# Attention visits between FFN steps regrouped into fewer and longer ones, and the transpose of q moved behind the sums

## Chip, cores and metric

One core of a Trainium2 chip. The metric is the device time of one execution in microseconds (us); a median and the range of a kernel's runs are given. All runs used here count as fast, with a mean granted TensorE clock of 0.992 to 1.0. Two of the traces, those of e1 and e2, hold a stretch of 3.4 us at half clock while PE works, and it matters below.

## The reference

Linformer attention feeds a max-out FFN. Eight batches, eight heads, sequence 1024, head size 64, 64 projected keys; then 8192 tokens of 512 go through three 512 x 768 matrices and one 768 x 512.

```python
k_proj = einsum('ks,bhsd->bhkd', E, k);  v_proj = einsum('ks,bhsd->bhkd', F, v)
attn = softmax(q @ k_proj^T / 8);        x = attn @ v_proj     # per batch and head
h = max(x @ w1, x @ w2, x @ w3);         out = h @ w_out
```

## The kernel before

TensorE (PE) runs the FFN of batch `b` as a loop of two halves, each of ten steps: 0 to 5 are "up" (12 matmuls of 128x128 by 512 columns), 6 to 9 "down" (6 such). The attention of the next batch `n = b + 1` is done in **visits** between those steps. A plan says which work stands behind which (half, step).

All PSUM is eight banks. The kernel deals them out; a score, sum or value unit takes a pair:

```python
    psum_t = psum.tile([P, 8, 512], FP32, name="banks")
    ...
    def two():                                  # a pair: 0-1, 2-3, 4-5 or 6-7
        n = min(range(0, 8, 2), key=lambda n: max(free[n:n + 2]))
    ...
    def bank():                                 # one bank: up, down, projections
        n = min(range(8), key=lambda n: free[n])
```

The pieces of a visit (cut):

```python
    sc(b, g)    # scores of head pair g: 4 matmuls 64x64 into a pair; ACT empties it with exp -> pT
    zc(b)       # column sums of all four pT; ACT makes 1/sum (zic); store to DRAM (zd),
                # four broadcast loads back (zi_all), all on the SyncE queue
    vx(b, g)    # values of pair g: 4 matmuls 64x64 into a pair; DVE empties it, times zi_all -> xT
    kproj(b), vproj(b)   # k, v projections, one bank each;  kt(b): transpose of k's, a pair
    qd(b)       # q: four copies on DVE (q_p), then one DMA transpose on the SyncE queue -> qT
    ld(b)       # loads of q, k, v; that of q waits until the transpose of the batch before landed
```

With `now=True` the exponential is put on ACT at once; otherwise it is put there after the next step's own copy. An up step takes three banks one after the other; ACT copies the first out, DVE takes the maxima with the second and third.

The plan from batch 3 on, before the change:

```python
        out = {
            (0, 1): [sc(n, 1, now=True), sc(n, 2, now=True), sc(n, 3)],
            (0, 3): [zc(n)],
            (1, 2): [vx(n, 0), vx(n, 1)],
            (1, 6): [vx(n, 2), vx(n, 3)],
        }
        if n + 1 < B:
            out[0, 2] = [qd(n + 1)]
            out[1, 2] = [kproj(n + 1), vproj(n + 1)] + out[1, 2]
            out[1, 3] = [kt(n + 1)]
            out[1, 6] += [sc(n + 1, 0)]
```

No visit has more than three units.

The softmax here doesn't subtract the row's maximum and nothing guards it: scores larger than these inputs give would overflow.

Of the kernel before, what the change touches and what calls it, by code (L numbers as in the profile page):

```python
# [15 lines left out]
def kernel(  # L16
# [15 lines left out]
    B, H, S, D = q.shape  # L32
# [10 lines left out]
    NPAIR = H // 2  # L43
# [38 lines left out]
    def bank():  # L82
        n = min(range(8), key=lambda n: free[n])
        deal((n,))
        return psum_t[:, n, :], (n,)

    def pe(dt, wait=0.0):
        clock["pe"] = max(clock["pe"], wait) + dt
        return clock["pe"]

    def runs(eng, ready, dt, ns=()):
        if eng in clock:
            clock[eng] = max(clock[eng], ready + 0.06) + dt
            for n in ns:
                free[n] = clock[eng]
            return clock[eng]
        return ready + dt
# [145 lines left out]
    def zi_all(b):  # L243
        if b not in zi_alls:
            zi_alls[b] = att.tile([P, NPAIR, 2, CHUNK], FP32, name="zi_all", bufs=1)
        return zi_alls[b]

    def zc(b):



        def f():
            t, ns = bank()
            for hp in range(2):
                for g in range(NPAIR):
                    nc.tensor.matmul(  # L256
                        out=t[32 * g:32 * (g + 1), :], lhsT=pick[:, hp, :],
                        rhs=pTs[b, g, 0][:, hp, :], start=(hp == 0), stop=(hp == 1),
                    )
            ready = pe(2 * MM + 0.1)  # L260
            zlc = att.tile([P, CHUNK], FP32, name="zlc", bufs=1)
            nc.scalar.activation(out=zlc, in_=t, func=AF.Ln)
            runs("s", ready, 0.6, ns)
            zic = att.tile([P, CHUNK], FP32, name="zic", bufs=1)
            nc.scalar.activation(out=zic, in_=zlc, func=AF.Exp, scale=-1.0)
            when = runs("s", ready, 0.63) + 9.0
            zd = scratch.tile([NPAIR, 2, 2, CHUNK], FP32, name="zd")
            nc.sync.dma_start(
                out=zd.rearrange("g h c f -> (g h c) f"),
                in_=zic.rearrange("(a r) f -> a r f", r=8)[:, 0, :],  # L270
            )
            for u in range(2):
                gs = slice(2 * u, 2 * u + 2)
                for hp in range(2):
                    nc.sync.dma_start(
                        out=zi_all(b)[hp * HALF:(hp + 1) * HALF, gs],
                        in_=zd[gs, hp].partition_broadcast(HALF),
                    )
            for g in range(NPAIR):
                zis[b, g, 0] = zi_all(b)[:, g], when  # L280
        return f

    def vx(b, g):
        def f():
            scale_x(b, g, 0, SI, values(b, g, 0, SI))
        return f
# [13 lines left out]
    def values(b, g, lo, nsi):  # L300
        if b not in xTs:
            xTs[b] = att.tile([P, NCT, SI, P], BF16, name="xT")
        return pair_mm(b, g, lo, nsi, lambda rows, hp: vps[b][rows, 2 * g + hp, :])
# [17 lines left out]
    def sc(b, g, lo=0, nsi=SI, now=False):  # L321
        def f():
            t = scores(b, g, lo, nsi)
            if now:
                exps(b, g, lo, nsi, t)
            else:
                later.append(lambda: exps(b, g, lo, nsi, t))
        return f

    def za(b, g, lo=0, nsi=SI, then=False):  # L330
        def f():
            z = sums(b, g, lo, nsi)
            av = values(b, g, lo, nsi)
            invert(b, g, lo, nsi, z)
            if then:
                later.append(lambda: scale_x(b, g, lo, nsi, av))
            else:
                scale_x(b, g, lo, nsi, av)
        return f
# [40 lines left out]
    def qd(b, parts=1):  # L380

        def f():
            q_p = att.tile([P, NPAIR, SI, 2, D], BF16, name="q_p", bufs=1)
            qTs[b] = att.tile([P, NPAIR * SI, P], BF16, name="qT")
            n = NPAIR // parts
            for lo in range(0, NPAIR, n):
                for g in range(lo, lo + n):
                    copy(
                        "v", q_p[:, g].rearrange("p si h d -> p h si d"),
                        qkv[b][0][:, 2 * g:2 * g + 2], (), 0.43,  # L390
                    )
                last_T[b] = nc.sync.dma_start_transpose(
                    out=qTs[b][:, lo * SI:(lo + n) * SI, :],
                    in_=q_p[:, lo:lo + n].rearrange("p g si h d -> p (g si h d)"),
                )
        return f

    kps = {}
    def kproj(b):
        def f():  # L400
            t, ns = bank()
            proj(b, 1, t, (LO, HI), 4 * D)
            kps[b] = att.tile([P, 2, 2 * D], BF16, name="kp")
            copy("v", kps[b].rearrange("a g x -> a (g x)"), t[:, 0:4 * D], ns, 0.43)
        return f

    def kt(b):
        def f():
            t, ns = two()
            t = t.bitcast(BF16)[:, 0]  # L410
            for gg in range(2):
                nc.tensor.transpose(
                    out=t[:, gg * P:(gg + 1) * P], in_=kps[b][:, gg, :], identity=ident
                )
            pe(0.2)

            kpTs[b] = att.tile([P, NPAIR, KP], BF16, name="kpT")
            copy(
                "v", kpTs[b].rearrange("a (y x) k -> a x y k", x=2),
                t[:, 0:2 * P].rearrange("a (x y k) -> a x y k", x=2, y=2), ns, 0.3,  # L420
            )
        return f

    def vproj(b):
        def f():
            t, ns = bank()
            proj(b, 2, t, (LO, HI), 4 * D)

            vps[b] = att.tile([P, H, D], BF16, name="vp")
            for hh, hs in enumerate((LO, HI)):  # L430
                i = t[hh * HALF:(hh + 1) * HALF, 0:4 * D].rearrange("a (h d) -> a h d", d=D)
                for to in range(2):
                    copy("sv"[hh], vps[b][to * HALF:(to + 1) * HALF, hs, :], i, ns, 0.4)
        return f
# [250 lines left out]
    def plan(b):  # L685
        n = b + 1
        if b == 0:
            c1 = (SPC, SPC)
            return {
                (0, 6): [za(0, 1, *c1), sc(0, 3, *c1)],  # L690
                (0, 7): [qd(1, 2), za(0, 2, *c1)],
                (0, 8): [za(0, 3, *c1)],
                (1, 0): [kproj(1)],
                (1, 1): [kt(1)],
                (1, 2): [vproj(1), ld(2)],
                (1, (3, "mid")): [sc(1, 0), sc(1, 1)],
                (1, 4): [za(1, 0), sc(1, 2)],
                (1, 5): [za(1, 1), sc(1, 3)],
                (1, 7): [za(1, 2)],
                (1, 8): [za(1, 3)],  # L700
            }
        if b == 1:
            return {
                (0, 1): [qd(2)],
                (0, 5): [kproj(2), vproj(2), ld(3)],
                (0, 6): [kt(2)],
                (0, 7): [sc(2, 0)],
                (0, 9): [za(2, 0), sc(2, 1)],
                (1, 1): [za(2, 1), sc(2, 2)],
                (1, 3): [za(2, 2), sc(2, 3)],  # L710
                (1, 5): [za(2, 3)],
                (1, 6): [qd(3)],
            }
        if b == 2:
            return {
                (0, 0): [kproj(3), vproj(3), ld(4)],
                (0, 1): [kt(3)],
                (0, 2): [sc(3, 0, now=True), sc(3, 1)],
                (0, 4): [sc(3, 2, now=True), sc(3, 3)],
                (0, 6): [zc(3)],  # L720
                (0, 7): [qd(4)],
                (1, 3): [kproj(4), vproj(4), ld(5), vx(3, 0), vx(3, 1)],
                (1, 4): [kt(4)],
                (1, 6): [vx(3, 2), vx(3, 3), sc(4, 0)],
            }
        if n == B:
            return {}
        out = {
            (0, 1): [sc(n, 1, now=True), sc(n, 2, now=True), sc(n, 3)],
            (0, 3): [zc(n)],  # L730
            (1, 2): [vx(n, 0), vx(n, 1)],
            (1, 6): [vx(n, 2), vx(n, 3)],
        }
        if n + 1 < B:
            out[0, 2] = [qd(n + 1)]
            out[1, 2] = [kproj(n + 1), vproj(n + 1)] + out[1, 2]
            out[1, 3] = [kt(n + 1)]
            out[1, 6] += [sc(n + 1, 0)]
        if n + 2 < B:
            out[1, 3] += [ld(n + 2)]  # L740
        return out
# [61 lines left out]
```

## Time and profile before

| | before |
|---|---|
| time, median (range) | 404.61 us (403.92 to 404.71, 3 runs) |
| profiled span | 402.6 us |
| PE busy / DVE / ACT | 97% / 50% / 39% |
| batch 3, 4, 5, 6 (from first FFN weight load to the next batch's) | 47.59, 46.49, 46.72, 44.29 us |

PE is the bound, so what counts is each interval in which the FFN matmuls do not follow each other at 0.216 us. I read these intervals from single starts of weight loads, of which none is missing in the trace (2311), while 43 matmul records are. The view below is the timeline of the kernel before at (1,6) of batch 5 (start, length, engine, line, operation, tiles, count, idle time before and what ended it). Two value units and one score follow each other, and the FFN goes on at once. (In all timelines shown, rows that the reading doesn't need, mostly weight loads, are left out.)

```profile
308.66 0.63 PE L231 MATMUL banks<-pT,vp 64*64 64x512 bf16 x8
308.77 0.58 ACT L102 COPY o_sb<-banks 128x512 f32<-128x512 f32 x1 [2.67 <-PE banks L664]
309.12 0.39 PE L211 MATMUL banks<-qT,kpT 64*64 64x512 bf16 x4
309.66 0.81 PE L664 MATMUL banks<-wout_sb,hT 128*128 128x512 bf16 x3 [0.16 <-issue]
```

The 0.16 before the last line is a missing record: the weight load that belongs to it starts at 309.43.

### The profile page before, as it was taken

What the parts mean: (1) busy time and instruction counts of PE and PEld (TensorE: products, weight loads), DVE (VectorE), ACT (ScalarE), POOL (GpSimd) and SP (SyncE); (2) the same over time, 40 slices, a digit from 0 to 9 for tenths busy, and PEclk for the clock granted to TensorE, in tenths of its full rate; (3) what the DMA queues carried; (4) which work ended last, traced back from release to release, by engine and by line L of the source; (5) the groups of instructions that cost most, each with busy time, mean ns of one, the idle gap of its engine ahead of it and who ended that gap; (6) DMA issues with size and microseconds to landing.
All of it is one profiled execution on the core that took longest, in us unless ns stands there. A gap on an engine that the chain in (4) does not pass through costs nothing.

```text
span 402.6 us, 5752 instructions
## 1 busy us (share of the span) xinstructions
PE 389.0 (97%) x2268; PEld 177.0 (44%) x2311; DVE 203.2 (50%) x319; ACT 155.8 (39%) x244; POOL 31.4 (8%) x44
## 2 busy tenths in 40 slices
PE   7899999999999999999999999999999999999996
PEld 3444444344445445444444445444454444444443
DVE  2347754762655425836264534746167342745251
ACT  2431537624763452253323532245322533132322
POOL 7350002002000200200010000100000000000000
PEclk9999999999999999999999999999999999999999
DMA  9999999969917999999899779983860229020202
GB/s 150 203 205 207 225 208 144 229 156 135 255 30 186 153 187 213 214 221 203 156 244 248 180 152 244 243 202 62 181 180 2 105 51 261 5 106 0 104 2 104
DMA packets 65707, 63.98 MB, mean 159 GB/s; under 512 B 30528, under 2 KB 58688, under 8 KB 65680
## 3 DMA queue, kind: packets, MB, share of 16 engines
q0 software_dynamic: 28512, 28.31, 43.9%
q1 hardware_dynamic: 37024, 35.16, 33.4%
q8 instruction: 18, 0.29, 0.3%
q10 hardware_dynamic: 144, 0.13, 0.1%
q14 instruction: 9, 0.07, 0.1%
HBM read 67.63 MB, written 16.94 MB: 210 GB/s over the span
## 4 chain that ended last, share of the span: by engine, by line
PE 85%; DMA 5%; DVE 3%; ACT 3%; issue 2%; POOL 0%; SPq 0%; DVEq 0%; ACTq 0%; POOLq 0%
PE banks L567 56%; PE banks L664 18%; PE banks L345 3%; PE banks L231 3%; DMA zi_all<-zd 3%; DMA k_t<-in_k_dram 2%; PE banks L211 2%; DVE xT L308 2%; ACT zl L291 1%; ACT zi_all L297 1%; PE banks L256 1%; DVE hT L577 1%; ACT pT L222 1%; DMA zd<-zic 1%; PE banks L470 1%
## 5 line engine op out<-in xcount | busy, mean ns | idle before, releaser
L567 PE MATMUL banks<-xT,w_sb 128*128 128x512 bf16 x1119 | 254.7, 379 | 2.8 <-issue 1.1
L567 PEld LDWEIGHTS <-w_sb 128*128 128x128 bf16 x1152 | 109.8, 98 | 137.5 <-issue 10.1
L629 DVE TENSOR_TENSOR m<-banks,h1s 128x512 f32<-128x512 f32 x90 | 62.1, 690 | 125.9 <-ACT h1s L625 81.1
L625 ACT COPY h1s<-banks 128x512 f32<-128x512 f32 x90 | 52.6, 584 | 112.2 <-PE banks L567 109.3
L664 PE MATMUL banks<-wout_sb,hT 128*128 128x512 bf16 x369 | 85.6, 379 | 1.3 <-issue 0.8
L577 DVE TENSOR_TENSOR hT<-banks,m 128x512 bf16<-128x512 f32 x90 | 62.3, 692 | 10.7 <-PE banks L567 1.7
L664 PEld LDWEIGHTS <-hT 128*128 128x128 bf16 x378 | 35.7, 98 | 47.4 <-issue 4.8
L102 ACT COPY o_sb<-banks 128x512 f32<-128x512 f32 (+1 forms) x56 | 32.6, 582 | 58.5 <-PE banks L664 58.3
L308 DVE TENSOR_TENSOR xT<-banks,zi_all 128x1024 bf16<-128x1024 f32 x28 | 33.3, 1221 | 22.5 <-ACT zi_all L297 17.0
L222 ACT ACTIVATE pT<-banks 128x1024 bf16<-128x1024 f32 (+1 forms) x36 | 32.8, 932 | 24.1 <-PE banks L211 24.1
L200 POOL DMA_DIRECT2D q_t<-in_q_dram x7 | 6.1, 878 | 189.9 <-DMA qT<-q_p 87.0
L291 ACT ACTIVATE zl<-banks 128x512 f32<-128x512 f32 (+1 forms) x16 | 13.0, 810 | 9.8 <-PE banks L231 8.9
L345 PEld LDWEIGHTS <-efT 128*64 128x64 bf16 x224 | 11.6, 110 | 3.4 <-issue 3.0
L102 DVE CAST vp<-banks 64x256 bf16<-64x256 f32 (+1 forms) x18 | 7.1, 397 | 10.9 <-ACT vp L102 7.8
L102 ACT CAST vp<-banks 64x256 bf16<-64x256 f32 x14 | 5.1, 364 | 19.0 <-PE banks L345 18.9
L231 PE MATMUL banks<-pT,vp 64*64 64x512 bf16 (+1 forms) x144 | 11.8, 362 | 0.4 <-DVE vp L102 0.4
L211 PE MATMUL banks<-qT,kpT 64*64 64x512 bf16 (+1 forms) x144 | 11.5, 361 | 0.0
L102 DVE COPY q_p<-q_t 128x1024 bf16<-128x1024 bf16 x28 | 10.0, 419 | 0.0
L297 ACT ACTIVATE zi_all<-zl 128x1024 f32<-128x1024 f32 x8 | 8.5, 1057 | 0.3
L102 DVE COPY o_sb<-banks 128x512 f32<-128x512 f32 (+1 forms) x9 | 5.8, 653 | 4.5 <-PE banks L644 4.5
L441 PE MATMUL banks<-warm_f 128*128 128x512 f32 x8 | 6.6, 977 | 1.5 <-DVE warm_f L175 1.5
L200 POOL DMA_DIRECT2D k_t<-in_k_dram x7 | 6.1, 878 | 20.2 <-PE banks L345 19.9
(59 smaller groups left out, 119.7 us busy)
## 6 DMA issues: line engine op xcount, KB each, us to landing
out_dram<-o_sb SPq DMA_DIRECT2D x30, 512.0 KB, 6.8
zi_all<-zd SPq DMA_DIRECT2D x20, 512.0 KB, 8.6
q_t<-in_q_dram POOLq DMA_DIRECT2D x7, 1024.0 KB, 13.4
k_t<-in_k_dram POOLq DMA_DIRECT2D x7, 1024.0 KB, 15.8
v_t<-in_v_dram POOLq DMA_DIRECT2D x7, 1024.0 KB, 20.1
w_sb<-in_moe_w_dram POOLq DMA_DIRECT2D x5, 384.0 KB, 11.7
k_t<-in_k_dram POOLq DMA_DIRECT2D x2, 512.0 KB, 10.7
v_t<-in_v_dram POOLq DMA_DIRECT2D x4, 256.0 KB, 13.3
```

Of the source, the lines that this page charges most:

```text
L102: done = {"v": nc.vector.tensor_copy, "s": nc.scalar.copy, "g": nc.gpsimd.tensor_copy}[eng](out=o, in_=i)
L211: nc.tensor.matmul(out=t[c * HALF:(c + 1) * HALF, hp, 0:n * P], lhsT=kpTs[b][rows, g, :], rhs=qTs[b][rows, at:at + n, :], start=True, stop ...
L222: nc.scalar.activation(out=pTs[b, g, lo], in_=t, func=AF.Exp, scale=scale)
L231: nc.tensor.matmul(out=t[hp * HALF:(hp + 1) * HALF, c, 0:nsi * HALF], lhsT=w(rows, hp), rhs=p[rows, hp, :], start=True, stop=True,)
L291: nc.scalar.activation(out=zl, in_=t, func=AF.Ln)
L308: nc.vector.tensor_tensor(out=xTs[b][:, g, lo:lo + nsi, :].rearrange("a (c s) p -> a c (s p)", c=2), in0=t, in1=zi, op=ALU.mult,)
L345: nc.tensor.matmul(out=t[hh * HALF:(hh + 1) * HALF, 0:width], lhsT=efT[:, si, (kv - 1) * KP:kv * KP], rhs=qkv[b][kv][:, heads[hh], si, :], ...
L567: nc.tensor.matmul(out=h, lhsT=w_sb[i][:, ct, jt * P:(jt + 1) * P], rhs=xTs[b][:, ct, ch * SPC:(ch + 1) * SPC, :], start=(ct == first), st ...
L577: nc.vector.tensor_tensor(out=o, in0=h, in1=other, op=ALU.max)
L625: nc.scalar.copy(out=h1s, in_=h[0][0])
L629: nc.vector.tensor_tensor(out=m12, in0=h[1][0], in1=h1s, op=ALU.max)
L664: nc.tensor.matmul(out=o_ps, lhsT=hTs[b, ch][:, jt, tt * P:(tt + 1) * P], rhs=wout_sb[:, jt, :], start=(jt == 0), stop=(jt == NJT - 1),)
```

## The change

The intent: fewer visits, since each costs a fixed price. From batch 5 on the four scores are made in one visit, at (1,6) of the batch before; three of the four value units go together behind the k and v projections; the last batch's four value units are one visit; two visits of batch 0 become one; and the transpose of q goes behind the sums, so that the reciprocals go first on the SyncE queue.

```diff
-                (1, 7): [za(1, 2)],
-                (1, 8): [za(1, 3)],
+                (1, 7): [za(1, 2), za(1, 3)],
...
-        out = {
-            (0, 1): [sc(n, 1, now=True), sc(n, 2, now=True), sc(n, 3)],
-            (0, 3): [zc(n)],
-            (1, 2): [vx(n, 0), vx(n, 1)],
-            (1, 6): [vx(n, 2), vx(n, 3)],
-        }
-        if n + 1 < B:
-            out[0, 2] = [qd(n + 1)]
-            out[1, 2] = [kproj(n + 1), vproj(n + 1)] + out[1, 2]
-            out[1, 3] = [kt(n + 1)]
-            out[1, 6] += [sc(n + 1, 0)]
+        out = {(0, 3): [zc(n)]}
+        if n == 4:
+            out[0, 1] = [sc(n, 1, now=True), sc(n, 2, now=True), sc(n, 3)]
+        if n + 1 == B:
+            out[1, 6] = [vx(n, g) for g in range(NPAIR)]
+            return out
+        out[0, 4] = [qd(n + 1)]
+        out[1, 2] = [kproj(n + 1), vproj(n + 1), vx(n, 0), vx(n, 1), vx(n, 2)]
+        out[1, 3] = [kt(n + 1)]
+        out[1, 6] = [sc(n + 1, 0, now=True), vx(n, 3)]
+        out[1, 6] += [sc(n + 1, g, now=True) for g in (1, 2)] + [sc(n + 1, 3)]
```

(`za` is a sum unit and a value unit together.)

## The prediction

> **What bounds the kernel now.** I read first the page (busy shares and slices), then the chain of waits, then the timeline around each visit, then the waits of VectorE (DVE) and ScalarE (ACT). A place such as (1,6) is half 1 of a batch's FFN, behind step 6; steps 0 to 5 are up, 6 to 9 down. Batches are numbered from 0 by their FFN.
>
> ```profile
> PE 389.0 (97%) x2268; PEld 177.0 (44%) x2311; DVE 203.2 (50%) x319; ACT 155.8 (39%) x244; POOL 31.4 (8%) x44
> ...
> PEclk9999999999999999999999999999999999999999
> ...
> PE 85%; DMA 5%; DVE 3%; ACT 3%; issue 2%; POOL 0%; SPq 0%; DVEq 0%; ACTq 0%; POOLq 0%
> ```
>
> TensorE (PE) is busy 97% at full clock and makes 85% of the chain; the other engines are at half or less. From batch 3 on one period of the FFN loop (all of batch 4's, then batch 5's) takes 46.49 and 46.73 us in the windows view. Its 192 FFN matmuls start 0.216 us apart (single starts in the timeline), which is 41.5 us. So some 5 us a batch is attention work and its switches, and only that can change. What a visit costs shows in the timeline of a visit of three scores:
>
> ```profile
> 266.61 5.34 PE L567 MATMUL banks<-xT,w_sb 128*128 128x512 bf16 x24
> 271.88 0.84 PE L211 MATMUL banks<-qT,kpT 64*64 64x512 bf16 x12
> 272.66 1.04 PE L567 MATMUL banks<-xT,w_sb 128*128 128x512 bf16 x3
> ```
>
> 24 FFN matmuls from 266.61 would end their slots at 266.61 + 24 x 0.216 = 271.79, and the FFN resumes at 272.66: 0.87 us for three units (a unit is one pair's four 64x64 matmuls). The same reckoning from single starts gives 0.65 us for the visits of two value units (343.14, 352.86) and 0.44 for one score (95.61). Slope 0.216 us a unit, intercept **0.22 us a visit**. The switch from values to scores inside a visit is free: units follow each other at 0.22 us in the visit at 308.66. Some matmul records are missing just after visits, so I checked against the weight loads, which are complete.
>
> The one large stall in this part is in batch 3, where the broadcast reciprocals arrive late. The chain of waits there:
>
> ```profile
> 193.69 0.35 ACT o_sb L102
> 194.04 2.13 DMA zd<-zic
> 196.16 0.02 issue
> 196.18 0.60 SPq L275
> 196.78 0.05 issue
> 196.84 10.30 DMA zi_all<-zd
> ...
> 207.26 1.24 DVE xT L308
> 208.50 0.04 issue
> 208.54 0.27 PE banks L412 x2
> ```
>
> zic itself was ready at 185.8 (timeline of ACT), but its store was issued at 194.04: the SyncE queue was busy for 10.34 us with the transpose of q ahead of it. The FFN gap at the kt visit is 1.19 us here against 0.33 in batches 4 and 5: **0.87 us lost**.
>
> **What the skill says.** "TensorEngine Tiling (Array Packing)", Key Properties, says that changing the tiling mode drains TensorE. The trace agrees: weight loads sit idle 0.41 to 0.42 us before and after each switch, and the intercept is 0.22 us. "PSUM — Partial Sum Buffer", Specifications: 8 banks a partition; the kernel deals them as four pairs, and a score or value unit takes a whole pair. "TensorEngine Tiling", PSUM Bottleneck: tiling does not speed up PSUM evacuation. The trace agrees: a unit is made in 0.22 us and emptied by an exponential in 1.03 us or a multiply in 1.22 us. "DMA: Bandwidth & Descriptors", Issuing engines are not separate DMA queues, says transfers of all issuers interleave on the same 16 engines; the transpose, the load of q that its landing releases (issued 196.56, just before the broadcasts) and the slow 10.3 us fit.
>
> **The change part by part.** No instruction is added or removed, only its place.
>
> (1) Visits saved: (0,1) in batches 4, 5 and 6, and (1,2) in batch 6. 4 x 0.22 = **-0.9 us**, all on PE, which is the path.
>
> (2) Transpose of q behind the sums: store and broadcasts start some 8 us earlier in batch 3, land by about 202 (estimate from 12 to 16 us from store to last landing there), and are wanted at 205: **-0.9 us**. Batches 4 and 5 waited for nothing, so nothing more. The four q_p copies, though, move to behind step 4, just before the last up step. Timeline of DVE in batch 5 now:
>
> ```profile
> 276.20 1.42 DVE L102 COPY q_p<-q_t 128x1024 bf16<-128x1024 bf16 x4
> ...
> 281.29 0.69 DVE L577 TENSOR_TENSOR hT<-banks,m 128x512 bf16<-128x512 f32 x1
> 283.09 0.69 DVE L629 TENSOR_TENSOR m<-banks,h1s 128x512 f32<-128x512 f32 x1 [1.10 <-PE banks L567]
> 283.88 0.69 DVE L577 TENSOR_TENSOR hT<-banks,m 128x512 bf16<-128x512 f32 x1
> ```
>
> Between hT (end 281.98) and the next maximum (283.09) there are 1.10 us idle; four copies fill about 1.35. So the last hT comes some 0.2 us later, and the down step has no slack: its sixth weight load waits for that hT already (to 284.63) and its matmul is just in time. 3 x 0.2 = **+0.6 us**.
>
> (3) The visit at (1,6), batches 3, 4, 5: score, value, score, score, score, which is **five pairs of banks where there are four**. Times from the last matmul before it (308.35 in batch 5): units at 0.32, 0.56, 0.78, 0.99, 1.21 if nothing waits. The down step's own bank is copied by ACT from 0.43 to 1.01 (the o_sb copy at 308.77), so the fourth pair waits until about 1.06. The fifth needs a pair given back: the first exponential runs behind that copy, 1.0 to 2.03; the multiply of the value unit ends at about 2.2. So the fifth starts at about 2.05 in place of 1.21 to 1.3: **+0.8 us** each, +2.4. Today's visit has three pairs and does not wait.
>
> (4) Three value units at (1,2) in batches 3, 4, 5. Timeline of batch 5 now:
>
> ```profile
> 299.48 0.87 DVE L102 CAST vp<-banks 64x256 bf16<-64x256 f32 x2 [1.22 <-ACT vp L102]
> 300.38 2.36 DVE L308 TENSOR_TENSOR xT<-banks,zi_all 128x1024 bf16<-128x1024 f32 x2
> ...
> 302.65 0.68 DVE L629 TENSOR_TENSOR m<-banks,h1s 128x512 f32<-128x512 f32 x1
> ```
>
> With a third unit, six banks are in value units and one in the v projection (until 300.34) when the next up step begins at about 299.36. Its first product takes the last free bank; its second (due 300.22) waits for the projection's bank, 0.2 us; its third (due 301.27) for the first multiply's end at 301.60, 0.4 us; the kt visit, which needs a pair, for the second's at 302.73, some 0.1 us. **+0.7 us** each, +2.1. The later maximum (third multiply to 303.9) has caught up by the last up step, as there is about 1.2 us of DVE slack a step.
>
> (5) Batch 6, (1,6): four value units. The down step behind them needs a bank from the first multiply (about 0.78 to 2.0 on the same scale) where PE would be there at 1.37: **+0.7 us**.
>
> (6) Batch 0, (1,7): two sums and two values, four pairs, while two o_sb copies wait on DVE until 72.86. PE leaves later, but the chain to the next batch runs through ACT (zl, zi_all, zl, zi_all, 71.99 to 76.25) and the multiply to 77.50, and PE waits 0.33 us for that already. So the saved switch is not seen: about **+0.2 us**.
>
> Sum: -0.9 - 0.9 + 0.6 + 2.4 + 2.1 + 0.7 + 0.2 = +4.2, or 408.8 us. Small waits can be absorbed where PE would have waited anyway (the hT wait at 307.6 costs 0.22 us in batches 3 and 5), so I put the time at **408.2 us**.
>
> **The rivals.** *The banks come free in time*: then only (1), (2) stand, 404.6 - 1.8 + 0.6 = 403.4 us. For it: the three-pair visits now wait for no bank, and scores at (0,1) run beside maxima without loss. Against it: five pairs do not fit in four, and 1.03 us of exponential cannot be hidden in 0.9 us of units. *Only the five-pair visit waits*, the value visit finds its banks: 408.8 - 2.1 = 406.7 us. *DVE or ACT stays behind*: three exponentials stand ahead of the next o_sb copy, and the multiplies ahead of the maxima, so that further banks come late: two more waits of 0.4 us in each of three batches, about 411 us. Against it: after the visit, three down steps of 1.3 us give ACT time, and only one copy of 0.59 us falls in each. *The broadcasts late again*: the third value unit now needs all four of them at (1,2), and the k and v loads still run in batch 3 until 192.9. Up to 1 us more.
>
> **Range and chances.** The low end, 404.4, has the value visit free and half of the wait in the five-pair visit; the high end, 410.4, has one more wait per batch. I choose 408.2 between the second rival and the sum. Two per cent is 8.1 us: slower needs 412.7, twice the sum; faster needs 396.5, more than all switches in these batches. Chances: faster 0.01, within 2% 0.96, slower 0.03.
>
> **What would show it.** In the changed profile: FFN gaps in the timeline of PE. The (1,6) visit should take about 2.1 us from FFN to FFN beyond its slot, not 1.3, with the last four scores of line 211 starting where an exponential (L222) ended; PE waits named after ACT pT or DVE xT at line 211; gaps of 0.2 to 0.4 us inside the up step after (1,2), ended by DVE vp or DVE xT; the kt gap of batch 3 without its zi_all wait; the zd store issued near 186 in place of 194; later hT waits before the first down step. It is wrong if PE shows no waits for banks at these visits, or if the transpose, now behind the broadcasts, delays q so that the scores at (1,6) wait for it (about 15 us of slack by my reckoning).

## The result and the profile after

407.35 us median (407.20 to 408.96, 4 runs) against 404.66 (403.92 to 405.01, 4 runs) of the kernel before. The ratio is 1.0078, with a 95% interval of 1.0049 to 1.0107; a ratio is the mean time of one kernel's fast runs over that of the other's of the same rounds, so not quite the ratio of these medians. By the 2% verdict it is "same"; the interval says slower. The page of the kernel after, its busy line and its chain:

```profile
PE 392.9 (97%) x2311; PEld 177.8 (44%) x2311; DVE 203.3 (50%) x319; ACT 155.8 (38%) x244; POOL 31.4 (8%) x44
...
PE 80%; DMA 9%; DVE 5%; ACT 3%; issue 2%; SPq 0%; DVEq 0%; ACTq 0%
```

The counts are the same (the 43 records that were missing are there), DVE's and ACT's busy times too, yet DVE's share of the chain has gone from 3 to 5%: PE waits for it more. (DMA's 9% is a load in the first 7 us and, in batch 0, the load of v from 25.3 to 55.5 us, which is on the chain of e5 too, a kernel that is faster than the one before.)

Where the time went, batch by batch:

| | before | after | difference |
|---|---|---|---|
| to the first FFN weight load | 19.98 | 18.34 | -1.64 |
| batch 0 | 55.10 | 56.00 | +0.90 |
| batch 1 | 47.97 | 47.64 | -0.33 |
| batch 2 | 49.27 | 49.27 | 0.00 |
| batch 3 | 47.59 | 49.03 | +1.44 |
| batch 4 | 46.49 | 47.91 | +1.42 |
| batch 5 | 46.72 | 48.15 | +1.43 |
| batch 6 | 44.29 | 43.92 | -0.37 |
| batch 7, to its last FFN weight load | 41.45 | 41.45 | 0.00 |

The first row is chance: nothing differs there, and over the profiles of this study the first FFN weight load starts at 18.3 to 20.0 us, and at 20.8 in e1, where the clock fell during the start. From there on the change costs **4.5 us**. Batch 3 also holds three units more than before and batch 6 three fewer (3 x 0.216 = 0.65 us), which cancels in the sum.

Three places carry it. The timeline of the kernel after at (1,6) of batch 5, five units on four pairs:

```profile
310.64 0.41 PE L211 MATMUL banks<-qT,kpT 64*64 64x512 bf16 x4
310.74 0.58 ACT L102 COPY o_sb<-banks 128x512 f32<-128x512 f32 x1 [2.67 <-PE banks L664]
310.88 0.39 PE L231 MATMUL banks<-pT,vp 64*64 64x512 bf16 x4
311.09 0.70 PE L211 MATMUL banks<-qT,kpT 64*64 64x512 bf16 x8
311.23 2.86 ACT L222 ACTIVATE pT<-banks 128x1024 bf16<-128x1024 f32 x3
311.32 1.23 DVE L308 TENSOR_TENSOR xT<-banks,zi_all 128x1024 bf16<-128x1024 f32 x1 [1.06 <-PE banks L231]
312.31 0.41 PE L211 MATMUL banks<-qT,kpT 64*64 64x512 bf16 x4 [0.52 <-ACT pT L222]
312.65 0.82 PE L664 MATMUL banks<-wout_sb,hT 128*128 128x512 bf16 x3
```

Read down: four units start by 311.4 (the fourth waited a little, for the o_sb copy). The fifth starts at 312.31, when the first of three exponentials, which started at 311.23 behind that copy, has given its pair back at 312.26. PE was idle for 0.52 us by the record, and the fifth unit stands 0.93 after the fourth in place of 0.22.

At (1,2) of batch 5 the kernel before has two value units, and PE goes through the next up step and the kt transposes without a wait:

```profile
299.38 2.54 PE L567 MATMUL banks<-xT,w_sb 128*128 128x512 bf16 x11 [0.16 <-issue]
301.75 0.27 PE L412 MATMUL banks<-ident,kp 128*128 128x128 bf16 x2
```

The timeline of the kernel after at the same place, with three value units:

```profile
299.53 0.84 PE L231 MATMUL banks<-pT,vp 64*64 64x512 bf16 x12
300.31 2.07 PE L567 MATMUL banks<-xT,w_sb 128*128 128x512 bf16 x8
300.42 0.87 DVE L102 CAST vp<-banks 64x256 bf16<-64x256 f32 x2 [1.22 <-PE banks L231]
301.32 3.49 DVE L308 TENSOR_TENSOR xT<-banks,zi_all 128x1024 bf16<-128x1024 f32 x3
301.34 0.76 PEld L567 LDWEIGHTS <-w_sb 128*128 128x128 bf16 x5 [0.49 <-DVE vp L102]
302.59 1.02 PE L567 MATMUL banks<-xT,w_sb 128*128 128x512 bf16 x4 [0.21 <-DVE xT L308]
303.73 0.27 PE L412 MATMUL banks<-ident,kp 128*128 128x128 bf16 x2
```

The up step's second product (weight load at 301.34) waits for the casts out of the v projection's bank, its third (302.59) for the first multiply, and the kt transposes (303.73) for the second multiply. The bank that PE wants is freed by DVE each time. The casts and these two multiplies stand ahead of the third multiply in DVE's queue and run as long after the first value unit as they did before (the first multiply 1.79 us after it, in both traces), so it is not the third multiply's work that PE waits for, but the pair that its unit holds.

The timeline at (1,6) of batch 6, four value units; the next down step waits for the first multiply:

```profile
354.84 1.15 PE L231 MATMUL banks<-pT,vp 64*64 64x512 bf16 x16
355.31 3.49 DVE L308 TENSOR_TENSOR xT<-banks,zi_all 128x1024 bf16<-128x1024 f32 x3 [0.95 <-PE banks L231]
356.58 2.10 PE L664 MATMUL banks<-wout_sb,hT 128*128 128x512 bf16 x9 [0.59 <-DVE xT L308]
```

And the gain, in the SyncE queue of batch 3: the store and the four broadcasts stand ahead of the transpose now. The store went out at 194.04 before, when the transpose ahead of it held the queue.

```profile
184.74 0.55 SPq L268 DMA_DIRECT2D zd<-zic  x1
189.35 2.55 SPq L275 DMA_DIRECT2D zi_all<-zd  x4
192.01 12.16 SPq L392 DMA_TRANSPOSE qT<-q_p  x1
```

### The profile page after: what moved, and what is told of

Its sections match the earlier page's. It is cut to its first block, busy times and chain, and to the rows that moved or that the text cites. A ratio compares the mean times of both kernels' runs of the same rounds, so it can differ in the third digit from the quotient of the medians.

```text
span 405.4 us, 5809 instructions
## 1 busy us (share of the span) xinstructions
PE 392.9 (97%) x2311; PEld 177.8 (44%) x2311; DVE 203.3 (50%) x319; ACT 155.8 (38%) x244; POOL 31.4 (8%) x44
## 4 chain that ended last, share of the span: by engine, by line
PE 80%; DMA 9%; DVE 5%; ACT 3%; issue 2%; SPq 0%; DVEq 0%; ACTq 0%
PE banks L567 52%; PE banks L664 18%; DMA v_t<-in_v_dram 7%; DVE xT L308 3%; PE banks L345 3%; PE banks L231 2%; PE banks L211 1%; DMA ef_f<-in_F_dram 1%; ACT pT L222 1%; ACT zl L291 1%; PE banks L441 1%; PE banks L256 1%; DVE m L629 1%; DVE vp L102 1%; DVE hT L577 1%
## 5 line engine op out<-in xcount | busy, mean ns | idle before, releaser
L567 PE MATMUL banks<-xT,w_sb 128*128 128x512 bf16 x1152 | 258.1, 379 | 0.9 <-DVE xT L308 0.6
L664 PE MATMUL banks<-wout_sb,hT 128*128 128x512 bf16 x378 | 86.8, 380 | 0.8 <-DVE xT L308 0.6
L102 ACT COPY o_sb<-banks 128x512 f32<-128x512 f32 (+1 forms) x56 | 32.6, 582 | 55.2 <-PE banks L664 54.8
L211 PE MATMUL banks<-qT,kpT 64*64 64x512 bf16 (+1 forms) x144 | 12.4, 364 | 1.5 <-ACT pT L222 1.5
L211 PEld LDWEIGHTS <-kpT 64*64 64x64 bf16 x144 | 4.2, 105 | 8.6 <-issue 6.3
L345 PE MATMUL banks<-k_t,efT 128*64 128x256 bf16 x112 | 7.5, 276 | 0.0
```

The lines of the kernel that those rows point to most:

```text
L102: done = {"v": nc.vector.tensor_copy, "s": nc.scalar.copy, "g": nc.gpsimd.tensor_copy}[eng](out=o, in_=i)
L211: nc.tensor.matmul(out=t[c * HALF:(c + 1) * HALF, hp, 0:n * P], lhsT=kpTs[b][rows, g, :], rhs=qTs[b][rows, at:at + n, :], start=True, stop ...
L345: nc.tensor.matmul(out=t[hh * HALF:(hh + 1) * HALF, 0:width], lhsT=efT[:, si, (kv - 1) * KP:kv * KP], rhs=qkv[b][kv][:, heads[hh], si, :], ...
L567: nc.tensor.matmul(out=h, lhsT=w_sb[i][:, ct, jt * P:(jt + 1) * P], rhs=xTs[b][:, ct, ch * SPC:(ch + 1) * SPC, :], start=(ct == first), st ...
L664: nc.tensor.matmul(out=o_ps, lhsT=hTs[b, ch][:, jt, tt * P:(tt + 1) * P], rhs=wout_sb[:, jt, :], start=(jt == 0), stop=(jt == NJT - 1),)
```

## The experiments

Theory: the merged visits ask for more bank pairs than there are, so PE waits for ACT or DVE to empty one; a saved visit is worth 0.22 us and each such wait 0.7 to 0.8. Rivals: the visits are merely longer because they hold more; ACT and DVE are behind there whatever the banks; the waits come from the moved transpose. All runs gave correct results. Timed ratios are against the kernel before of the same rounds; a ratio's interval is 0.3 to 0.6% wide, 1.3 to 2.5 us, so single parts are read from batch lengths in the traces, which repeat to a few hundredths of a microsecond where no late transfer and no fall of the clock is involved.

| run | time, median us | ratio (95%) | batch 3 | 4 | 5 | 6 |
|---|---|---|---|---|---|---|
| before | 404.66 | 1 | 47.59 | 46.49 | 46.72 | 44.29 |
| after | 407.35 | 1.0078 (1.0049 to 1.0107) | 49.03 | 47.91 | 48.15 | 43.92 |
| e9, after again | 407.61 | 1.0094 (1.0068 to 1.0120) | 49.02 | 47.91 | 48.14 | 43.92 |
| e1 | 407.19 | 1.0068 (1.0042 to 1.0094) | 47.56 | 47.33 | 47.57 | 44.80 |
| e6 | 405.51 | 1.0036 (1.0020 to 1.0053) | 48.44 | 47.33 | 47.56 | 43.92 |
| e7 | 409.22 | 1.0136 (1.0110 to 1.0162) | 49.63 | 48.52 | 48.77 | 43.92 |
| e10 | 405.94 | 1.0062 (1.0031 to 1.0093) | 48.44 | 47.32 | 47.56 | 43.42 |
| e2 | 408.99 | 1.0133 (1.0104 to 1.0162) | 51.10 | 47.30 | 47.54 | 44.29 |
| e3 | 402.88 | 0.9975 (0.9955 to 0.9996) | 46.75 | 46.51 | 46.77 | 44.29 |
| e4 | 404.08 | 1.0002 (0.9980 to 1.0025) | 47.59 | 46.49 | 46.72 | 44.29 |
| e5 | 402.57 | 0.9964 (0.9949 to 0.9980) | 46.72 | 46.49 | 46.72 | 44.29 |
| e8 | 404.67 | 1.0016 (0.9991 to 1.0041) | 48.54 | 46.72 | 46.96 | 44.29 |

### e1: the scores back at (0,1)

```diff
-        if n == 4:
+        if n >= 4:
             out[0, 1] = [sc(n, 1, now=True), sc(n, 2, now=True), sc(n, 3)]
-        out[1, 6] = [sc(n + 1, 0, now=True), vx(n, 3)]
-        out[1, 6] += [sc(n + 1, g, now=True) for g in (1, 2)] + [sc(n + 1, 3)]
+        out[1, 6] = [vx(n, 3), sc(n + 1, 0)]
```

> The changed kernel with scores 1 to 3 of the next batch put back to (0,1), so that (1,6) holds one value unit and one score: three kinds of work less in one visit, one visit more in batches 4, 5 and 6. Theory (five pairs do not fit in eight banks): the gap at (1,6) falls from about 2.1 us beyond the slot to 0.65, no PE wait for ACT pT is left, and each of batches 3, 4 and 5 loses a wait of some 0.8 us; three visits come back at 0.22. Against the changed kernel -2.4 + 0.66 = -1.7 us, about 405.7. Rival (the (1,6) visit is long only because it does more work): the visit gets shorter by its units alone, the batches keep their length but for the visit that came back: +0.7 us, about 408.0.

Measured: batches 4 and 5 0.58 us shorter than in the changed kernel, which is -0.80 for the wait and +0.22 for the visit that came back. Batch 3 lost 1.47 (0.82 and three units of 0.216), batch 6 gained 0.88 (0.22 and the three units). The sum is -1.75 us, as the theory had it; the rival's +0.7 is ruled out. The timed median, 407.19, is above the 405.7 expected, and its ratio does not differ from the changed kernel's by itself. The profiled run's first FFN weight load started at 20.75 us, the latest of all, against 18.34 in the trace of the changed kernel. Its granted clock was 0.50 from 9.73 to 13.15 us, in the start, so much of the gain was lost there. Three of the four runs have a mean clock of 0.994 to 0.996; the fourth, at 1.0, took 405.94 us, close to the 405.7 expected.

### e6: the five units in two visits

```diff
-        out[1, 6] = [sc(n + 1, 0, now=True), vx(n, 3)]
-        out[1, 6] += [sc(n + 1, g, now=True) for g in (1, 2)] + [sc(n + 1, 3)]
+        out[1, 6] = [sc(n + 1, 0, now=True), vx(n, 3), sc(n + 1, 1)]
+        out[1, 8] = [sc(n + 1, 2, now=True), sc(n + 1, 3)]
```

> The changed kernel with the five-pair visit cut in two: score 0, value 3 and score 1 at (1,6), scores 2 and 3 at (1,8). Same units between the same two up steps, only one more switch. Theory (banks): no wait in either, one switch of 0.22 us more, so -0.8 + 0.22 = -0.6 us in each of batches 3, 4 and 5: -1.7 us against the changed kernel, about 405.6. Rival (ACT and DVE are simply behind there, so that what comes later waits in any case): the wait moves to (1,8) or to the next up step, and the batch keeps its 47.9 us or grows by 0.2.

Measured: -0.59, -0.58, -0.59 us, so 0.80 of wait less 0.22 for a visit. The same five units between the same two up steps cost less in two visits than in one. The wait did not move to (1,8), which speaks against "ACT and DVE are behind anyway".

### e7: the copy ahead of the exponentials twice

```diff
         copy(eng, o_sb[:, tt % 2, :], o_ps, ns)
+        if 3 <= b < 6 and (ch, tt) == (1, 0):
+            nc.scalar.copy(out=o_sb[:, tt % 2, :], in_=o_ps)
```

> The changed kernel with the o_sb copy that stands on ACT ahead of the exponentials at (1,6) made twice, in batches 3, 4 and 5 (same data, right result). Theory (the fifth pair waits for the first exponential, which waits for this copy): the fifth unit and the FFN behind it come one copy, 0.58 us, later in each of three batches: +1.7 us against the changed kernel, about 409.1. Rival (the fifth unit waits for the multiply on DVE, or PE's wait has another cause): under 0.2 us a batch, about 407.6.

Measured: +0.60, +0.61, +0.62 us a batch. The timeline of this run at (1,6) of batch 5 shows the chain: copy, second copy, exponential, fifth unit. The fourth unit (312.94) waits for the second copy too, which holds its bank.

```profile
311.69 0.59 ACT L102 COPY o_sb<-banks 128x512 f32<-128x512 f32 x1 [2.69 <-PE banks L664]
312.31 0.59 ACT L674 COPY o_sb<-banks 128x512 f32<-128x512 f32 x1
312.79 2.86 ACT L222 ACTIVATE pT<-banks 128x1024 bf16<-128x1024 f32 x3
312.94 0.41 PE L211 MATMUL banks<-qT,kpT 64*64 64x512 bf16 x4 [0.52 <-ACT o_sb L674]
313.87 0.41 PE L211 MATMUL banks<-qT,kpT 64*64 64x512 bf16 x4 [0.52 <-ACT pT L222]
```

The path of the visit's end is ACT's. The rival with the multiply on DVE is out: with the second copy the fifth unit still waited for the exponential, which ended at 313.83, while the multiply ended at 313.48. PE could not take the multiply's pair instead, since the kernel deals the pairs when the program is built; with a choice at run time the second copy would have cost some 0.35 us less (an estimate from these two ends).

### e10: the merged value visits cut

```diff
-            out[1, 6] = [vx(n, g) for g in range(NPAIR)]
+            out[1, 6] = [vx(n, g) for g in range(3)]
+            out[1, 8] = [vx(n, 3)]
...
-        out[1, 2] = [kproj(n + 1), vproj(n + 1), vx(n, 0), vx(n, 1), vx(n, 2)]
+        out[1, 2] = [kproj(n + 1), vproj(n + 1), vx(n, 0), vx(n, 1)]
+        out[1, 4] = [vx(n, 2)]
```

> The changed kernel with its two merged value visits cut: in batches 3 to 5 the third value unit leaves (1,2) for a visit of its own at (1,4), and in batch 6 the fourth leaves (1,6) for (1,8). The five-pair visit stays. Theory (the up step behind (1,2) finds no bank; the down step behind four value units finds none): batches 3, 4 and 5 lose 0.8 us of waits and pay 0.22 for a visit, -0.6 each; batch 6 loses 0.7 and pays 0.22, -0.5; -2.3 us against the changed kernel, about 405.2. Rival (the kt visit and the multiplies on DVE set the pace of the up steps there, whatever the banks): -0.2 us or less a batch.

Measured: -0.59, -0.59, -0.59 in batches 3 to 5 and -0.50 in batch 6. So the third unit at (1,2) costs 0.81 us of waits, and the fourth at (1,6) of batch 6 0.72. DVE does the same multiplies, one of them a visit later, so the sum of its work is not what PE waits for; together with the order in DVE's queue (above) this leaves the banks.

### e2: the third value unit alone, on the kernel before

```diff
         if n + 1 < B:
+            out[1, 2], out[1, 6] = [vx(n, 0), vx(n, 1), vx(n, 2)], [vx(n, 3)]
```

> The kernel before with one thing of the change: the third value unit done at (1,2) in place of (1,6), in batches 3, 4 and 5. Theory (banks of the next up step): two FFN waits and a later kt visit, 0.8 us in batches 4 and 5 as in the changed kernel; in batch 3 the wait for the late broadcasts is there already and covers it. +1.6 us against before, about 406.3. Rival (the waits after (1,2) in the changed kernel come from its other moves, such as the later transpose): 0, about 404.7.

Measured: +0.81 and +0.82 in batches 4 and 5, as expected, but **+3.51 in batch 3**, where I had expected the old stall to cover it. Two things add up there. First the granted clock of this run, from its page (40 slices of 10.2 us), then its timeline in batch 3:

```profile
PEclk9999999999999999999989999999999999999999
...
207.18 2.36 DVE L308 TENSOR_TENSOR xT<-banks,zi_all 128x1024 bf16<-128x1024 f32 x2 [1.89 <-DMA zi_all<-zd]
208.45 1.02 PE L567 MATMUL banks<-xT,w_sb 128*128 128x512 bf16 x4 [2.08 <-DVE xT L308]
...
209.75 3.44 PE L567 MATMUL banks<-xT,w_sb 128*128 128x512 bf16 x8
```

- The wait. With three value units the up step's third product (208.45) needs the pair of the first multiply, and that multiply waits for the first two of the four broadcasts, which had landed by 207.05. The product starts 2.45 us after the weight load before it, against 0.59 in batches 4 and 5: 1.86 us, where the kernel before loses 0.87 at its kt visit. So the old stall does not cover the third unit's waits, as I had expected; it grows with them.
- The clock. From 209.48 to 212.89 us the granted clock is 0.50, and the eight matmuls from 209.75 take 3.37 us in place of 1.73: 1.64 us. The clock fell one microsecond after PE's wait of 2.08 us had ended; whether the wait brought it on, no run here shows.

The third multiply waited for the last broadcasts until 211.84, but in this trace no FFN matmul behind the kt visit waited for it. (How late the broadcasts land is partly chance, as e8 shows below.) So in batch 3 the earlier broadcasts are worth 0.87 us by themselves, and about 1.9 once the third value unit is moved: the two parts of the change belong together. The timed ratio of e2 includes such falls of the clock in part: its four runs have mean clocks of 0.992 to 0.999.

### e3 and e5: the transpose of q alone, at (0,4) and at (0,7)

```diff
-            out[0, 2] = [qd(n + 1)]
+            out[0, 4] = [qd(n + 1)]        # e3;  e5: out[0, 7]
```

> The kernel before with the transpose of q alone moved from (0,2) to (0,4). Theory: the store of the reciprocals in batch 3 goes out near 186 us on the profile's clock in place of 194, the 0.87 us stall at the kt visit goes; the down step's first wait for hT grows by under 0.1 us in three batches. -0.8 us, about 403.8. Rival (my prediction's +0.2 us a batch for the copies on DVE): -0.3 us, about 404.4.

> The kernel before with the transpose of q at (0,7), in the down steps where DVE has little to do. Theory: the whole 0.87 us of batch 3 and no later hT: -0.9 us, about 403.8, the fastest so far. Rival (the transpose comes too late: the score at (1,6) or the load of q waits for it): a wait on qT at line 211 in the trace, 404.7 or more.

Measured: e3 -0.84 in batch 3, +0.02 and +0.05 in batches 4 and 5; e5 -0.87, 0.00, 0.00. No score waited for qT in e5. The intervals of the timed ratios, 0.9975 and 0.9964, lie below 1, so both are faster than the kernel before, by less than the 2% of the verdict. The timed gains, 1.0 and 1.5 us, are larger than 0.87; the stall that they remove varies by chance (e8), and the start adds its own. **e5 has the lowest median of this study, 402.57 us**: it keeps the part that paid without a wait and leaves the visits as they were.

### e4: the merged visit of batch 0 alone

```diff
-                (1, 7): [za(1, 2)],
-                (1, 8): [za(1, 3)],
+                (1, 7): [za(1, 2), za(1, 3)],
```

> The kernel before with the merged visit of batch 0 alone. Theory (four pairs and two o_sb copies that still hold banks; the chain to batch 1 is ACT's): the saved switch is not seen, and batches 0 and 1 together grow by 0.2 to 0.5 us, about 405.0. Rival (a switch saved is a switch saved): -0.2 us, about 404.4.

Measured: no difference in time (0.9980 to 1.0025). In the steps around the merged visit the trace shows +1.38, -0.86, +0.20 and -0.32 us, +0.4 in sum. All seven profiles with this edit show these four differences, and none of the four without it does. Whole batches don't show it cleanly: batch 0 takes 54.8 to 56.2 us over these profiles, as it absorbs chance in the first loads (0.18 us of the +0.90 in the changed kernel is a wait for the load of v, ahead of the merged visit). So the timing rules out more than 1 us either way and no more; that the saved switch is not seen rests on the steps.

### e8: one visit more, on the kernel before

```diff
-            out[1, 6] += [sc(n + 1, 0)]
+            out[1, 8] = [sc(n + 1, 0)]
```

> The kernel before with the score unit of (1,6) taken out and made at (1,8), in batches 3 to 5: one visit more, same work, and no visit with more than three pairs. Theory (a visit has a fixed price of 0.22 us): each of these three batches grows by 0.22 us, +0.65 us in all, about 404.7 beside 404.0. Rival (the intercept of my line through visits of one, two and three units is not the price of a visit): no growth.

Measured: +0.23 and +0.24 in batches 4 and 5: the price of a visit. Batch 3 grew by 0.95, of which 0.72 is a longer wait for the broadcasts. That wait lies ahead of this edit's first difference, in a program that is the same up to there, so it is chance of the transfers; it also shows how fragile that stall is.

### e9: the changed kernel again

> The changed kernel as it is, again, on the chip of this call. The traces so far put the change at +4.5 us from the first FFN matmul on, while the timed runs gave +3.2 us (interval 2.0 to 4.3); the first FFN matmul starts anywhere between 18.3 and 20.8 us in the profiles of kernels whose starts are the same. Theory (start differs by chance, the rest is fixed): batches 3, 4, 5 take 49.0, 47.9, 48.1 us again to within 0.05, and the timed ratio lies between 1.008 and 1.012. Rival (the trace overstates it): batches shorter than in the first trace.

Measured: batches 3 to 6 within 0.01 us of the first trace, ratio 1.0094. The trace's +4.5 us lies at the top of the second interval (1.0068 to 1.0120 is 2.7 to 4.8 us) and just above that of the first. So the direction and the parts are settled; the total is 3 to 4.5 us, and the trace does not settle how much of the rest the start's chance takes.

## Why the prediction was right

The time, 407.35 us, lies in the range; the point, 408.2, was 0.85 high, on a sum of 408.8. The mechanism was right in its two main steps, (3) and (4). That the sum agrees with the measured parts to 0.1 us is in part luck: the q copies were put 0.5 us too high, and the value visits and batch 0 together 0.5 too low. The parts, with the run that measured each:

| part | predicted | measured | from |
|---|---|---|---|
| (1) four visits saved | -0.9 | 4 x -0.22 = -0.9 | e1; e8: 0.23 |
| (2) broadcasts before the transpose | -0.9 | -0.87 | e5 |
| (2) q copies later on DVE | +0.6 | +0.07 | e3, batches 4 and 5 |
| (3) five pairs at (1,6) | +2.4 | 0.82 + 0.80 + 0.80 | e1, e6, e7 |
| (4) third value unit at (1,2) | +2.1 | 3 x 0.81 = +2.4 | e10, e2 |
| (5) four value units in batch 6 | +0.7 | +0.72 | e10 |
| (6) batch 0 | +0.2 | +0.4 | e4, steps of the trace |
| sum | +4.2 | +4.3 | trace: +4.5, with 0.18 of chance in batch 0 |

- **The central step held**: five pairs do not fit in four, and the fifth unit waits for an exponential that itself waits for a copy. I had its start 2.05 us after the last FFN matmul; the trace has 312.31 - 310.31 = 2.0.
- **The value visit held too**, with the three waits by name: DVE vp, DVE xT, and the kt pair. In batch 5 they cost 0.16, 0.38 and 0.27 us, where I had 0.2, 0.4 and 0.1; the kt visit makes it 0.1 us a batch larger than I had it.
- **The q copies were mis-sized.** The step "the down step has no slack" was wrong. The sixth weight load does wait for hT longer (0.35 us idle before it in batch 5, 0.20 before the change), but in the kernel before it stood 0.13 us ahead of its matmul (284.63 and 284.76), and this took up most of the delay: 0.02 to 0.05 us a batch was left.
- **Batch 0** was 0.2 us dearer: the second value unit there waited for ACT's first logarithm (zl; in batch 0 ACT makes the reciprocals from the sums), not for the o_sb copies. PE waits 0.76 us for it in the trace.
- **The rivals.** "The banks come free in time" (403.4) is out by e1, e6 and e10. "Only the five-pair visit waits" is out by e10. "DVE or ACT stays behind" (411) is out by e6 and e10, where the waits did not move to later steps. "The broadcasts late again" did not happen in the changed kernel; e2 shows what they cost a third value unit without the moved transpose: 1.86 us of wait in place of 0.87, so the 1 us more that I allowed, if the stretch of half clock is set aside. q did not delay the scores, though the slack was 8.5 us in batch 3 (landed 206.13, first score 214.58) and about 11 in the others, not the 15 I reckoned.
- **Shading.** I put the point 0.6 below the sum because small waits might be absorbed. The trace gives no such absorption. The pair of profiled runs differs by 2.9 us because the changed kernel's start was 1.64 us shorter by chance; that the point lies nearer to the time than the sum does is luck.
- **A reading.** The weight loads do not sit idle for 0.41 to 0.42 us at each switch: from the k and v projections to values it is 0.20, and behind a wait for hT 0.23 or 0.34. No part of the sum rests on it.

## What to carry to other kernels

Before merging work into fewer, longer visits, count what the merged visit holds of the scarcest buffer at once, and who empties it how fast: here a switch costs 0.22 us, and one unit beyond the banks costs 0.8, because a pair is filled in 0.22 us and emptied in over 1. Look also one step past the visit, since the work behind it needs buffers too. When an effect is under 1%, read it from the length of repeated stages in the trace, after a look at the granted clock in each: in e2 nearly half of the growth of batch 3 was a stretch of half clock. Put transfers that someone waits for ahead of those that nobody waits for.

## What the Trainium skill lacked or had wrong

- "TensorEngine Tiling (Array Packing)", Key Properties, says that a mode switch drains TensorE but gives no price. Here a visit in 64x64 mode between 128x128 matmuls costs 0.22 us for both switches together (fit over visits of one, two and three units; 0.23 and 0.24 when one more visit was added). Going from values to scores within 64x64 mode costs nothing: units still start 0.22 us apart.
- "TensorE: Matmul & The Clock Gate", Back-to-back issue gap, gives about 131 ns a matmul for a sustained stream of weight load and matmul at 512 columns. Here no two FFN matmuls of 512 columns start less than 0.215 us apart, in any of the traces; the section's formula for the isolated gap (512/2.4 + 2.5 = 216 ns) is what fits. (Elsewhere the same page gives 215.7 ns for back-to-back matmuls, which agrees.)
- "DMA: Bandwidth & Descriptors", Issuing engines are not separate DMA queues, calls the sequencer's time to start a DMA usually small. The DMA transpose of q held the SyncE queue for 4.8 to 12.6 us in these traces, and what stood behind it on that queue waited as long; in batch 3 that order was worth 0.87 us.
- No page has a rule for how many PSUM units a stretch may hold: "PSUM — Partial Sum Buffer" gives the eight banks, and the rates at which the engines read stand on other pages, but none sets the two against each other. Here a pair is filled in 0.22 us and emptied in 1.03 (exponential on ScalarE) or 1.22 us (multiply on VectorE) for 128 x 1024 fp32 elements, and one unit beyond the banks cost 0.8 us.
